# Second MLP product of a sixth round in three one-pass products, with a new order of all engines

## The chip, the cores and the metric

One core of one Trainium2 chip runs the kernel. The metric is the time of one execution in microseconds (us), as the median of several runs. Beside it stands one profiled execution, whose trace gives the start and the duration of each instruction on the five engines: PE (TensorE, matrix products), DVE (VectorE), ACT (ScalarE), POOL (GpSimd) and SP (SyncE, which here only issues transfers).

## What is computed

The reference is a linear attention followed by an MLP over each token:

```
# attention, per batch b and head h, with a state of 48 x 48
for t in range(S):                       # S = 768
    y[t] = r[t] @ (state + outer(u * k[t], v[t]))
    state = w[t][:, None] * state + outer(k[t], v[t])
# the 8 heads of 48 side by side give x: (4, 768, 384)
xn = (x - mean(x)) / sqrt(var(x) + 1e-6) * g_ln
out = x + maximum(xn @ w_ch1, 0) @ w_ch2     # w_ch1: 384 x 1536, w_ch2: 1536 x 384
```

All of it is in FP32.

## The kernel before

The work is cut into 8 rounds (`NR`), each of one batch and 384 of its tokens. A round has a *front*, the attention, and a *back*, the MLP.

**The front** forms products of decays in blocks that double in length (`quads`, `grow`, `keep`; tiles `k`, `r`, `tot`, and `A` for the 64 x 64 blocks of attention weights), most of it elementwise work on DVE with many small matrix products on PE between. The operands arrive as `nat_w`, `nat_k`, `nat_r` and `v`; `inner` multiplies them on DVE or POOL into `pad_k`, `pad_r`, `nat_k` and `nat_r`. At the end of a front `states` scans the states (`s`, and `last` for the next round; 10 small DVE instructions per group of four heads), `outputs` multiplies them with `r` on PE, and a copy by ACT or DVE leaves the round's rows in `x`.

**The back** normalises `x`, turns it (`xT_ps`, `xf`), and for 12 slabs `f` of the hidden layer forms `h` (`h_ps`, ReLU by ACT). Two ways of forming a product are used:

- FP32 as the engine has it. It is used for the first product of round 0 (`first_product`, tiles `w1` and `xf`), and for the second product (`o`, against `ffn2`) of the rounds below `LAST`: 3 row tiles times 12 slabs, 36 products per round.
- Three products in `fp32r`, one pass each. Both operands are split into a high and a low part, and into a scaled difference of the two, each exact in the shorter format (names ending in `H`, `L`, `D`). It is used for the first product of rounds 1 to 7 (parts `xhl` and `xd`, or `xk` and `xr`, against `wh`, `wl` and streamed `d`), and for the second product of the rounds from `LAST` on (`thirds`: 108 products per round, with `hH` by ACT, `hL` by DVE or POOL, `hD` by DVE, against the parts of `w_ch2` that `halve2` forms once as `w2H`, `w2L`, `w2D`).

`LAST` is 3, so rounds 3 to 7 use `thirds`. The parts of `w_ch2` are 36 slabs of 128 x 384 and have no room of their own. `w2_place` puts them into buffers that the fronts leave: `k`, `r`, `A`, `v`, `vx`, `tot`, `nat_k`, `nat_r` (tags `k`, `r`, `A`, `v`, `vx`, `tot`, `nk`, `nr`). Therefore the first `thirds` product of a round waits until the fronts of all rounds are done:

```
            if first:
                need += x_of(NR - 1)
```

The rounds' `x` lie in four buffers; `x_tag` puts that of round 7 into the buffer of `nat_w`. `h` has 12 buffers (tag `h`).

**The order.** `Plan.order` goes through a list of numbers, `ORDER`, one for each step of the kernel. It fixes the order of the instructions on every engine, and for steps that two engines can do (`EITHER`) the ten-thousands pick the engine. No engine reorders anything. Where the list leaves PE without a ready step for over 0.35 us by the plan's own account, `order` puts in products of zeros (`idle`), in whole pieces of 128 columns:

```
            if idle and e == "PE" and t - free["PE"] > 0.35:
                early = max(min(t - 0.1, self.WARMED) - free["PE"], 0.0)
                n = int(early / idle[1] / 2 + (t - 0.1 - free["PE"] - early) / idle[1])
```

All engine calls pass through one helper, so the profile names line 47 for nearly all of them; the tiles' names tell them apart.

Of the kernel before, what the change touches and what calls it, by code (L numbers as in the profile page):

```python
# [63 lines left out]
class Plan:  # L64
# [294 lines left out]
def kernel(  # L359
# [140 lines left out]

    BY = {"DVE": DVE, "POOL": POOL}
    EITHER = ("DVE", "POOL")
    THREE, LAST = 1, NR - 5

    def at(rnd, stage):
        return 40 * rnd + stage
# [617 lines left out]
    def x_tag(rnd):  # L1124
        return "x" if rnd < NR - 1 else "nw"
# [279 lines left out]
    def w2_place(n, f):  # L1405
# [4 lines left out]
        if f < 6:  # L1410
            return ("nk", "nr")[f - 4], f"xw2_{f}", 3, i
# [413 lines left out]
```

## Time and profile before

| what | us |
|---|---|
| median of 3 runs | 469.05 (468.63 to 470.08) |
| the profiled execution, its own time | 469.36 |
| its span, first to last instruction | 467.6 |
| PE busy | 459.7 (98%) |
| DVE busy | 352.5 (75%) |
| ACT busy | 264.5 (57%) |
| POOL busy | 139.1 (30%) |

The own time exceeds the span by 1.76 us, for what lies before the first and behind the last instruction. The span can be read in two parts: up to about 300 us the fronts run, with backs of rounds 0 to 3 between them; behind that PE does one-pass products alone. A PE that is shown busy can still be slow, since the records of a product overlap the next one; what a product costs is read from the distance of the starts.

### The profile page before, as it was taken

How to read it: one execution, taken by the hardware profiler on the slowest of the kernel's cores; microseconds unless marked ns; L12 is line 12 of the kernel's file. 1: busy time of each engine (PE TensorE's matmuls, PEld its weight loads, DVE VectorE, ACT ScalarE, POOL GpSimd, SP SyncE). 2: the span in 40 equal slices, each digit the busy share in tenths (PEclk: the TensorE clock that was granted, in tenths of full speed). 3: DMA queues.
4: the chain of work that ended last, by engine and by line, in shares of the span. 5: the costliest groups of instructions: out<-in, count | busy, mean ns of one | idle time of the engine just before them, and what ended most of it. 6: DMA issues, size and time to landing. Idle time of an engine off the chain costs nothing.

```text
span 467.6 us, 17460 instructions
## 1 busy us (share of the span) xinstructions
PE 459.7 (98%) x7442; PEld 400.8 (86%) x7442; DVE 352.5 (75%) x742; ACT 264.5 (57%) x608; POOL 139.1 (30%) x141
## 2 busy tenths in 40 slices
PE   9999999999999999999999999999999999999996
PEld 5766888766899766899766899999999999999996
DVE  8999899999997768897879887976633535525535
ACT  4697889754674332665621678855555455544440
POOL 4237014322361152363443230221013122321030
PEclk9999999999999999999999999999999999999999
DMA  7889765885657606844630545312212232142011
GB/s 207 248 199 240 203 124 144 239 212 139 180 160 162 133 4 151 185 128 127 170 66 4 86 123 133 105 32 69 84 55 70 80 102 67 37 135 68 35 50 51
DMA packets 105501, 56.23 MB, mean 120 GB/s; under 512 B 61904, under 2 KB 102352, under 8 KB 105424
## 3 DMA queue, kind: packets, MB, share of 16 engines
q1 hardware_dynamic: 105152, 54.92, 45.9%
q8 instruction: 58, 0.95, 0.9%
q10 hardware_dynamic: 272, 0.20, 0.1%
q14 instruction: 19, 0.16, 0.1%
HBM read 45.27 MB, written 7.47 MB: 113 GB/s over the span
## 4 chain that ended last, share of the span: by engine, by line
PE 86%; DVE 6%; DMA 3%; ACT 2%; POOL 2%; issue 1%; DVEq 0%; SPq 0%; POOLq 0%; ACTq 0%
PE h_ps L47 28%; PE a L47 25%; PE o L47 15%; PE o_2P L47 4%; PE idle L47 3%; PE r_ps L47 2%; PE k_ps L47 2%; PE o_2D L47 2%; DMA raw<-in_moe_w_ch_dram 2%; PE kn_ps L47 2%; PE xT_ps L47 2%; DVE s L47 1%; ACT held L47 1%; DMA va<-own_d 1%; POOL nat_k L47 1%
## 5 line engine op out<-in xcount | busy, mean ns | idle before, releaser
L47 ACT ACTIVATE h<-h_ps 128x384 f32<-128x384 f32 (+2 forms) x108 | 47.9, 457 | 50.5 <-PE h_ps L47 49.8
L47 PE MATMUL o<-ffn,h 128*128 128x384 f32 x216 | 74.6, 491 | 0.0
L47 DVE SCALAR_TENSOR_TENSOR hD<-hH,hL 128x384 fp32r<-128x384 f32 x60 | 36.4, 617 | 37.1 <-POOL hL L47 16.0
L47 POOL TENSOR_TENSOR hL<-h,hH 128x384 fp32r<-128x384 f32 x28 | 30.2, 1084 | 102.7 <-PE a L47 27.7
L47 ACT ACTIVATE h_ps<-h_ps 128x384 f32<-128x384 f32 x84 | 39.7, 480 | 34.5 <-PE h_ps L47 33.4
L47 PEld LDWEIGHTS o<-ffn,h 128*128 128x128 f32 x216 | 39.2, 190 | 23.0
L47 PEld LDWEIGHTS a<-r,k 48*56 48x56 f32 (+3 forms) x3072 | 40.0, 122 | 10.8 <-issue 5.2
L47 PE MATMUL h_ps<-xd,d 128*128 128x384 f32 x204 | 47.1, 335 | 0.0
L47 PE MATMUL a<-r,k 48*56 48x32 f32 (+3 forms) x3072 | 44.2, 208 | 1.0 <-issue 0.7
L47 PE MATMUL h_ps<-xhl,wl 128*128 128x384 f32 x180 | 40.4, 334 | 0.0
L47 DVE TENSOR_TENSOR r<-r,tot 112x768 f32<-112x768 f32 (+1 forms) x40 | 32.3, 809 | 9.6 <-PE a L47 9.6
L47 PE MATMUL h_ps<-xhl,wh 128*128 128x384 f32 x180 | 39.1, 326 | 0.0
L47 DVE TENSOR_TENSOR k<-k,tot 112x768 f32<-112x768 f32 (+1 forms) x40 | 31.6, 791 | 6.7 <-PE a L47 4.7
L47 ACT ACTIVATE hH<-h 128x384 fp32r<-128x384 f32 x60 | 29.7, 519 | 11.6 <-PE a L47 7.8
L47 PEld LDWEIGHTS h_ps<-xd,d 128*128 128x128 f32 x204 | 34.0, 189 | 0.5
L47 DVE TENSOR_TENSOR hL<-h,hH 128x384 fp32r<-128x384 f32 x32 | 18.0, 569 | 20.0 <-PE a L47 9.5
L47 PEld LDWEIGHTS h_ps<-xhl,wh 128*128 128x128 f32 x180 | 30.8, 189 | 0.0
L47 PE MATMUL idle<-nought 128*128 128x384 f32 (+2 forms) x90 | 29.6, 452 | 0.9 <-DVE eps L47 0.9
L47 ACT COPY A<-a 32x384 f32<-32x384 f32 (+5 forms) x56 | 23.6, 422 | 11.9 <-DVE xhl L47 5.6
L47 PEld LDWEIGHTS h_ps<-xhl,wl 128*128 128x128 f32 x180 | 30.1, 189 | 0.2
L47 PE MATMUL a<-w2D,hD 128*128 128x384 f32 x90 | 29.7, 330 | 0.4 <-DVE hD L47 0.4
L47 ACT ACTIVATE xf<-xT_ps,g_sb 128x384 f32<-128x384 f32 (+2 forms) x27 | 14.7, 550 | 22.1 <-PE xT_ps L47 19.0
(184 smaller groups left out, 1136.9 us busy)
## 6 DMA issues: line engine op xcount, KB each, us to landing
d<-w1d SPq DMA_DIRECT2D x84, 192.0 KB, 2.6
raw<-in_moe_w_ch_dram SPq DMA_DIRECT2D x24, 384.0 KB, 4.6
nat_w<-in_w_dram SPq DMA_DIRECT2D x24, 192.0 KB, 4.0
nat_r<-in_r_dram SPq DMA_DIRECT2D x24, 192.0 KB, 4.0
v<-in_v_dram SPq DMA_DIRECT2D x24, 192.0 KB, 4.1
nat_k<-in_k_dram SPq DMA_DIRECT2D x23, 192.0 KB, 4.1
out_dram<-x SPq DMA_DIRECT2D x15, 192.0 KB, 2.0
w1d<-w1diff SPq DMA_DIRECT2D x12, 192.0 KB, 2.3
```

Of the source, the lines that this page charges most:

```text
L47: ins = self.tc.keep_in_program_order(f(*args, **kw))
```

## The change

- `LAST` becomes 2: round 2 too uses `thirds`. Its second product is 108 one-pass products in place of 36 FP32 products; its `h` is split by ACT, DVE and POOL; each of its three row tiles gets two additions on DVE in place of one, and its rows are stored by three transfers in place of one.
- The buffer of `nat_k` takes `x` of round 6, so that rounds 2 to 7 all have room for `x` while they wait. The parts of slab 4 of `w_ch2` that stood there move to three buffers of the tag `h`, which leaves nine for `h` itself.
- The parity in `x_places` follows `LAST`: rounds 3, 5 and 7 put their parts into `xk` and `xr`, before it was rounds 4 and 6.
- `ORDER` is another list, so that every engine has another order, and some steps another engine.

```
     ORDER = [
-        10008, 3, 2, 10012, 4, 9, 10, 5, 11, 16, 264, 261, 7, 14, 13, 18, 10019, 262, 17, 265, 260, 263,
...
+        4, 3, 2, 11, 7, 9, 10, 12, 13, 5, 263, 260, 261, 262, 16, 10018, 19, 264, 265, 269, 14, 17, 21,
...
     EITHER = ("DVE", "POOL")
-    THREE, LAST = 1, NR - 5
+    THREE, LAST = 1, NR - 6
...
     def x_tag(rnd):
-        return "x" if rnd < NR - 1 else "nw"
+        return {NR - 2: "nk", NR - 1: "nw"}.get(rnd, "x")
...
         if f < 6:
-            return ("nk", "nr")[f - 4], f"xw2_{f}", 3, i
+            return ("nr", "xw2_5", 3, i) if f == 5 else ("h", f"w2{n}_4", 1, 0)
```

260 rows, old and new, of the table ORDER are left out of this document.

## The prediction

> **What bounds the kernel now.** I read the page first: the span, the busy times and the slices.
>
> ```profile
> span 467.6 us, 17460 instructions
> PE 459.7 (98%) x7442; PEld 400.8 (86%) x7442; DVE 352.5 (75%) x742; ACT 264.5 (57%) x608; POOL 139.1 (30%) x141
> PE   9999999999999999999999999999999999999996
> DVE  8999899999997768897879887976633535525535
> PE 86%; DVE 6%; DMA 3%; ACT 2%; POOL 2%; issue 1%; DVEq 0%; SPq 0%; POOLq 0%; ACTq 0%
> ```
>
> PE is busy everywhere and carries 86% of the chain that ended last, so the kernel is bound by PE. But the DVE slices show a second candidate: 9 nearly throughout the first 12 slices (140 us), 7 and 8 until about 300 us, then 3 to 6. Next I cut the span into stages by windows (PE, PEld, DVE, ACT, POOL busy, then PE's granted clock); the cuts at 297.4 and 299.7 us are explained below.
>
> ```profile
> 0.00:10.00 10.00, 9.07 (x22) 5.41 (x23) 7.73 (x24) 4.15 (x5) 5.33 (x16) 1.00 0.69 203
> 10.00:60.00 50.00, 47.95 (x1043) 37.72 (x1042) 47.73 (x117) 40.17 (x102) 17.03 (x17) 1.00 0.82 216
> 60.00:140.00 80.00, 80.00 (x1513) 64.70 (x1511) 77.96 (x160) 57.49 (x136) 27.60 (x24) 1.00 0.68 175
> 140.00:297.40 157.40, 157.29 (x3730) 129.17 (x3724) 129.53 (x276) 78.64 (x177) 53.72 (x51) 1.00 0.50 114
> 299.70:463.00 163.30, 162.88 (x1013) 161.49 (x1005) 85.69 (x162) 81.74 (x186) 35.28 (x33) 1.00 0.22 66
> ```
>
> From 60 to 140 us DVE is busy 77.96 of 80 us (97.5%); from 140 to 297.4 us 129.53 of 157.4 (82%): there PE's products set the pace and DVE has slack. Behind the fronts DVE needs 85.69 of 163.3 us, half. So there are two regimes, a front stage with two engines near their limit and a back stage of PE alone. The timeline gives the hinges: the last state scan on DVE, the last attention product on PE, PE's last product, and the last addition.
>
> ```profile
> 296.82 0.61 DVE L47 SCALAR_TENSOR_TENSOR s<-s,decay,a 112x48 f32<-112x48 f32 x3
> 299.34 0.46 PE L47 MATMUL a<-s,r 48*64 48x48 f32 x18
> 462.89 0.33 PE L47 MATMUL a<-w,hH 128*128 128x384 f32 x1
> 463.95 0.62 DVE L47 SCALAR_TENSOR_TENSOR x<-a,rstd,x 128x384 f32<-128x384 f32 x1
> ```
>
> DVE ends the scans at 297.4 us, PE the fronts at 299.7 us (2.3 later), PE its last product at 463.1 us (163.4 later), and 4.5 us remain for additions and the store. 299.7 + 163.4 + 4.5 = 467.6. The change is costed as a shift of the first two terms.
>
> **The product itself.** From the chain in order of time, for the price of one product, and from the groups of line, engine and form, for the fillers:
>
> ```profile
> 239.84 3.89 PE o L47 x12
> 440.31 3.90 PE h_ps L47 x24
> L47 PE MATMUL o<-ffn,h 128*128 128x384 f32 x216 | 74.6, 491 | 0.0
> L47 PE MATMUL idle<-nought 128*128 128x384 f32 x44 | 20.2, 582 | 0.9 <-DVE eps L47 0.9
> ```
>
> An FP32 product leaves two records (216 for 3 rounds of 36), so 12 records in 3.89 us are 6 products of 0.648 us. A one-pass product leaves one record: 24 in 3.90 us, 0.1625 us each. Round 2 gives up 36 x 0.648 = 23.3 us and takes 108 x 0.1625 = 17.55 us: PE gains 5.8 us.
>
> **Fillers.** The changed order holds 54 products of zeros (116 pieces of 128 columns), before 45 (97 pieces). A piece is a third of a 384-column FP32 product, 0.216 us: 19 more cost 4.1 us. Where they stand matters more. Before, all lie ahead of PE's first `h_ps`. Now 23 pieces, at nine places, stand in the middle, from the end of round 1's `o` to round 6's products with `A`: the order itself finds no product there, since round 2's second product, which could fill, must now wait for the last front. The code puts in whole pieces and leaves 0.1 to 0.34 us at each place, so 0.9 to 3.1 us of waiting stay uncovered; I take 2.
>
> **What moves.** Counted in the two orders, PE has this ahead of the last attention product: `o` products 108 before, 72 after; one-pass `h_ps` 318 before, 210 after (round 3 had 102 of its 108 there; now only round 2's stand there, less a last piece); transposes 9 fewer, about 1 us; attention products equal. So 23.3 + 108 x 0.1625 + 1.0 - 4.1 = 37.7 us less PE work ahead of that hinge, and 216 x 0.1625 + 1.0 = 36.1 us more behind it. By PE alone the fronts end at 299.7 - 37.7 + 2 = 264.0 us.
>
> DVE is the question, for the fronts are the same work and must fit into that shorter stage. Until the last scan it was busy 7.73 + 47.73 + 77.96 + 129.53 = 263.0 us. The largest differences of its list until that scan, with these prices:
>
> ```profile
> L47 DVE COPY_PREDICATED A<-mask,a 128x768 f32<-128x768 int8 x18 | 17.9, 992 | 4.6 <-PE a L47 4.6
> L47 DVE TENSOR_TENSOR nat_r<-pad_k,pad_r 128x576 f32<-128x576 f32 x9 | 7.9, 882 | 0.4 <-POOL pad_r L47 0.4
> L47 DVE SCALAR_TENSOR_TENSOR x<-o,rstd,x 128x384 f32<-128x384 f32 x9 | 5.4, 609 | 2.1 <-PE o L47 2.1
> L47 DVE COPY x<-a 128x288 f32<-128x288 f32 x11 | 5.0, 451 | 1.1 <-PE a L47 1.1
> L47 DVE TENSOR_TENSOR nat_k<-nat_k,nat_r 128x1152 f32<-128x1152 f32 x3 | 4.1, 1352 | 0.1
> L47 DVE TENSOR_SCALAR xn<-x,mv 128x384 f32<-128x384 f32 x8 | 3.2, 415 | 0.0
> L47 DVE TENSOR_TENSOR pad_k<-nat_k,nat_w 128x576 f32<-128x576 f32 x2 | 1.5, 748 | 0.0
> ```
>
> Three masked copies, three `nat_r`, three `x<-o`, five `x<-a` and five `xn` go (to ACT, to POOL, or behind the scan): 2.98 + 2.65 + 1.83 + 2.26 + 2.08 = 11.8 us. Four `nat_k` products and four `pad_k` products come from POOL: 5.41 + 2.99 = 8.4 us. The other differences are a few instructions of each of two dozen kinds, by estimate 5 to 9 us fewer. That leaves 263.0 - 8.3 to 263.0 - 12.4: 250.6 to 254.7 us of DVE work. After the first 10 us (7.73 busy, loads arriving) 242.9 to 247.0 us remain. At the 97.5% of the 60-to-140 stage they take 249.1 to 253.3 us, the scan ends at 259.1 to 263.3 us, and PE's last attention product at 261.4 to 265.6 us. At 95.5%, the 47.73 of 50 us of the stage before, it is 266.6 to 270.9 us; with DVE never idle 255.2 to 259.3 us, and then PE's 264.0 holds.
>
> So both engines want 264 us, each to run there without slack, and each waits for the other: PE gets scans and masked copies from DVE, DVE gets blocks from PE. Before, neither had to: DVE idled 18% in the longer half of the fronts. I take 265.0 us, one more than PE's figure, inside DVE's band.
>
> **The burst behind the fronts.** `thirds` starts almost at once now: 1.3 us of PE work after the last attention product, 5.2 before. It needs splits of `h` and of `w2`, about 0.55 us from start to start:
>
> ```profile
> 301.98 0.63 DVE L47 SCALAR_TENSOR_TENSOR w<-w,ffn 128x384 fp32r<-128x384 f32 x1
> 302.54 0.68 DVE L47 SCALAR_TENSOR_TENSOR w2L<-w2H,ffn 128x384 fp32r<-128x384 f32 x1
> DVE hD L47 <- POOL hL L47: 16.0, 8, 3.3
> L47 POOL TENSOR_TENSOR hL<-h,hH 128x384 fp32r<-128x384 f32 x28 | 30.2, 1084 | 102.7 <-PE a L47 27.7
> ```
>
> From the last scan to `hD` of slab 3 DVE has 21 instructions, 11.5 us; PE has 7.7 us of products ahead of that slab and starts 2.3 us later. It waits 1.5 us there; by slab 6 DVE has caught up. Before, slab by slab, PE's work exceeded DVE's, and the stage lost 2 us in all. I add 1 us: 163.4 + 36.1 + 1.0 = 200.5 us. If DVE also waits for POOL's `hL`, as 8 times before for 2 us each, it is up to 4 us more.
>
> **Hidden.** ACT's 12 more `hH`, three more additions and the three short stores lie in the back stage, where ACT is busy 81.74 and DVE 85.69 of 163.3 us. 5 of the 24 new `hL` and `hD` go to POOL. Nine buffers for `h` in place of 12 cost nothing while ACT splits each `h` soon; else PE waits for a free `h`. Round 6's rows must wait until round 7 has used up `nat_k`; that copy stands near the end of the fronts anyway. If these covers go, each costs its wait of 0.5 to 2 us.
>
> **The sum.** 265.0 + 200.5 + 4.5 = 470.0 us of span, 2.4 more than 467.6. Against its own time that is 471.8 (469.36 + 2.4), against the median of the runs 471.4 (469.05 + 2.4; the profiled execution stood 0.3 above it).
>
> **Rivals.** (1) *The gain comes through.* DVE runs gapless, the splits are ready, and the nine edges vanish, since the real waits are shorter than the plan's: PE's ledger alone, 262.0 + 199.5 + 4.5 = 466.0, so 467.4 at the median, or 466 if the front's fewer handovers save another 1 to 1.5 us. For: 97.5% was held for 80 us. Against: the order's own fillers say that PE has nothing to do. (2) *It cancels.* PE's ledger with its 2 us of edges, DVE just keeps up, the burst costs nothing: 264.0 + 199.5 + 4.5 = 468.0, 469.5 at the median. (3) *The burst decides, slower.* Fronts at 265.0, but `hD` waits for POOL and ACT in the first six slabs: 3 to 4 us on top, 475. It decides from the point where slab 6 still finds PE waiting. (4) *The clock falls in the thinned front.* The windows show a granted clock of 1.00 in every stage, so no stage here is slow; if it halved for the about 10 us around the fillers, of which by estimate half is products that PE must do, they would take some 5 us longer: 476. Against: fillers stand at just these places.
>
> The Trainium skill, page "TensorE: Matmul & The Clock Gate", section "HAM oscillation — how this bites in real kernels", warns of idle gaps over about 3.4 us, after which the clock is halved; by that rule the fourth rival needs one gap of that length, and the trace shows none so far.
>
> (5) That the change does not do what it says is excluded: the built order holds 648 one-pass `thirds` products, 540 before.
>
> **How the numbers follow.** Forecast 0.43, rival 1 0.22, rival 2 0.20, rival 3 0.12, rival 4 0.03. 0.3% (1.4 us) is about what a measurement of this kernel can tell from no change: faster means below 467.6, slower above 470.5. Rival 1 gives faster 0.20; rival 2, with the edges of 1 and of the forecast, gives 0.23 within; the rest, 0.57, is slower. The range goes from 465.5 (rival 1 with a little more) to 476.5 (DVE at 95.5%: 268.8 + 200.5 + 4.5 = 473.8, so 475.3; or the burst).
>
> **What would show it.** Right: the last attention product between 263 and 268 us; DVE at 96% or more until then; PE waiting for DVE or POOL between its fillers at 170 to 230 us and in the first slabs of round 2's `thirds`; then some 199 to 201 us of dense products. Wrong, faster: the fronts end by 262 us and DVE's idle share stays below 2%. Wrong, slower: waits for `h` buffers, or gaps, in the back stage, which I count as dense.

## The result, and the profile after

The changed kernel takes 480.8 us (median of four runs, 478.6 to 482.2) against 469.6 us before (four runs, one more than ahead of the prediction): a ratio of 1.0233, with a 95% interval of [1.0212, 1.0255]. All ratios leave out the runs of a second, slower state (three of the kernel before with less PE work, one of the version with eight waits). The prediction was 471.4, with a range up to 476.5. The profiled execution took 480.1 us by its own time, with a span of 478.4 us where 470.0 was predicted. From its page, in the order of the prediction:

```profile
span 478.4 us, 17626 instructions
PE 460.9 (96%) x7496; PEld 408.5 (85%) x7496; DVE 362.8 (76%) x751; ACT 281.4 (59%) x648; POOL 125.9 (26%) x141
PE   8998999999999989998998999999999999999996
DVE  6999999999996998999996994564733463542535
PE 67%; DVE 20%; ACT 5%; SPq 3%; DMA 2%; issue 2%; ACTq 0%; DVEq 0%
```

PE is no longer 9 throughout: five slices ahead of the hinge show an 8, and DVE is at 9 nearly until the fronts' end. Of the chain that ended last, PE carries 67% (86% before) and DVE 20% (6%). The *hinge* is the end of the fronts: the last state scan on DVE and, behind it, the last attention product on PE. The windows (PE, PEld, DVE, ACT, POOL busy, then the granted clock of PE):

```profile
10.00:60.00 50.00, 46.12 (x1021) 35.62 (x1020) 48.27 (x115) 42.41 (x105) 15.38 (x18) 1.00 0.83 225
60.00:140.00 80.00, 78.56 (x1463) 62.55 (x1463) 79.16 (x148) 54.07 (x129) 26.17 (x25) 1.00 0.68 169
140.00:200.00 60.00, 58.42 (x1554) 46.30 (x1546) 53.01 (x112) 29.11 (x66) 23.55 (x24) 1.00 0.55 130
200.00:272.40 72.40, 67.75 (x2089) 58.57 (x2082) 66.81 (x148) 45.13 (x103) 18.91 (x23) 1.00 0.45 98
275.50:474.10 198.60, 198.48 (x1238) 197.61 (x1230) 104.11 (x203) 102.46 (x235) 37.54 (x35) 1.00 0.23 68
```

The timeline's hinges: the last scan, the last attention product, the last product, the last addition.

```profile
270.88 1.49 DVE L47 SCALAR_TENSOR_TENSOR s<-s,decay,a 112x48 f32<-112x48 f32 x8
275.15 0.46 PE L47 MATMUL a<-s,r 48*64 48x48 f32 x18
473.91 0.33 PE L47 MATMUL a<-w,hH 128*128 128x384 f32 x1
474.97 0.62 DVE L47 SCALAR_TENSOR_TENSOR x<-a,rstd,x 128x384 f32<-128x384 f32 x1
```

The last scan ends at 272.4 us, the fronts on PE at 275.5, PE's products 198.6 us later, and 4.3 us remain. Predicted were 265.0 + 200.5 + 4.5. So the fronts are 10.5 us late, and the back stage is 1.9 us better than predicted; it is dense (198.48 of 198.60 us busy). All of the miss of this execution lies ahead of the hinge. Its granted clock is 1.00; two of the other three executions had a mean of 0.991 and 0.993 and took 482.2 and 481.5 us, while those at 1.000 took 480.1 and 478.6. So 1 to 2 us of the median may be the clock.

### The profile page after: what moved, and what is told of

Same layout as the page of the kernel before. It is cut to its first block, busy times and chain, and to the rows that moved or that the text cites. A ratio compares the mean times of both kernels' runs of the same rounds, so it can differ in the third digit from the quotient of the medians.

```text
span 478.4 us, 17626 instructions
## 1 busy us (share of the span) xinstructions
PE 460.9 (96%) x7496; PEld 408.5 (85%) x7496; DVE 362.8 (76%) x751; ACT 281.4 (59%) x648; POOL 125.9 (26%) x141
## 4 chain that ended last, share of the span: by engine, by line
PE 67%; DVE 20%; ACT 5%; SPq 3%; DMA 2%; issue 2%; ACTq 0%; DVEq 0%
PE h_ps L47 27%; PE a L47 23%; PE o_2P L47 5%; PE o L47 4%; DVE A L47 4%; DVE nat_k L47 3%; SPq L47 3%; DVE s L47 2%; PE o_2D L47 2%; DVE k L47 2%; DVE vals L47 2%; DVE r L47 1%; PE r_ps L47 1%; PE xT_ps L47 1%; DMA nat_r<-in_r_dram 1%
## 5 line engine op out<-in xcount | busy, mean ns | idle before, releaser
L47 POOL TENSOR_TENSOR hL<-h,hH 128x384 fp32r<-128x384 f32 x33 | 37.2, 1132 | 144.1 <-ACT hH L47 66.7
L47 PE MATMUL o<-ffn,h 128*128 128x384 f32 x144 | 50.6, 491 | 0.0
L47 DVE TENSOR_TENSOR hL<-h,hH 128x384 fp32r<-128x384 f32 x39 | 21.5, 554 | 27.8 <-ACT hH L47 15.7
L47 ACT ACTIVATE hH<-h 128x384 fp32r<-128x384 f32 x72 | 36.3, 520 | 6.1 <-PE a L47 3.1
L47 PE MATMUL a<-w2D,hD 128*128 128x384 f32 x120 | 39.3, 327 | 0.0
L47 PEld LDWEIGHTS o<-ffn,h 128*128 128x128 f32 x144 | 25.8, 190 | 14.0 <-ACT tot L47 0.2
L47 PE MATMUL a<-w2L,hL 128*128 128x384 f32 x108 | 35.2, 326 | 0.0
L47 PE MATMUL a<-w2H,hH 128*128 128x384 f32 x108 | 35.2, 326 | 0.0
L47 PE MATMUL h_ps<-xhl,wl 128*128 128x384 f32 x144 | 32.1, 332 | 0.3
L47 PE MATMUL h_ps<-xhl,wh 128*128 128x384 f32 x144 | 31.2, 326 | 0.0
L47 PEld LDWEIGHTS idle<-nought 128*128 128x128 f32 x108 | 18.9, 197 | 9.3 <-issue 1.5
```

The lines of the kernel that those rows point to most:

```text
L47: ins = self.tc.keep_in_program_order(f(*args, **kw))
```

## Experiments

Two theories came first: A, that DVE's work now sets the fronts' end; B, that PE's order and its handovers do. The differences in us below are the difference of the ratio from 1.0233 (changed kernel) or from 1 (before), times 469.6 us.

### Less DVE work, and less PE work

Edit in both kernels (the product `nat_k` x `u`):

```
-            k_, k_, lambda: u_bc[...]..., 2 * half, 5,
+            lambda: k_()[..., 0:1], lambda: k_()[..., 0:1], lambda: u_bc[...]...[..., 0:1], 2 * half, 5,
```

> The changed kernel, with the product nat_k x u on one element in 48 of each row (it leaves out most of the product with u). Seven of these run on DVE inside the fronts, 1.35 us each for 1152 columns; at 24 columns by estimate some 1.18 us less each, 8.3 us less DVE work. Theory A (after the change DVE's work sets the fronts' end): the last scan comes 6 to 8.3 us sooner, the last attention product too, and the time falls from 480.8 to 472.5 to 475. Theory B (PE's own order and its handovers set it): the hinge stays at 275, 480 to 481.

> The kernel before with the same cut (most of the product with u is left out): six on DVE, about 7.1 us less DVE work, and one on POOL. Theory A: DVE had slack in the fronts before, so the time falls by at most 1.5 us, 468 to 469.5. Theory B: the same nothing, 469.5. If it falls by 5 us or more, DVE was the bound before as well and theory A's contrast is false.

The group in the changed kernel:

```profile
L47 DVE TENSOR_TENSOR nat_k<-nat_k,u_bc 128x1152 f32<-128x1152 f32 x7 | 10.2, 1461 | 0.0
```

Its group with the cut, and the last scan on the timeline then:

```profile
L47 DVE TENSOR_TENSOR nat_k<-nat_k,u_bc 128x24 f32<-128x24 f32 x7 | 2.1, 301 | 0.0
```

```profile
268.32 1.48 DVE L47 SCALAR_TENSOR_TENSOR s<-s,decay,a 112x48 f32<-112x48 f32 x8
```

8.1 us of this group went (DVE's busy time until the last scan fell by 7.7), the last scan came 2.6 us sooner (269.8), the ratio is 1.0173 [1.0109, 1.0236], 2.8 us, or 5.8 at the interval's lower end. The kernel before moved by 1.0 us (0.9979 [0.9943, 1.0015]). Theory A as stated falls: by the middle a third came through, not 6 to 8.3 us.

Edit for PE in both kernels (the second product of round 1):

```
-                    for f_ in range(f, f + KC):
+                    for f_ in range(f, f + KC, 2 if rnd == 1 else 1):
```

> The changed kernel with half of round 1's second MLP product left out (every second slab's FP32 products, 12 of 0.648 us: 7.8 us less PE work in the fronts). Theory A: DVE sets the fronts' end, the hinge moves by 0 to 3 us, time 478 to 481. Theory B: the hinge moves by all of it, time 473.

> The kernel before with the same half of round 1's second product left out (7.8 us less PE work in the fronts). Both theories: PE sets the fronts' end there, the time falls by 6 to 7.8 us, to 462 to 463.5. If it falls by less than 4 us, DVE was close behind PE before the change too.

Neither kernel gained: 1.0239 [1.0151, 1.0326] and 1.0009 [0.9971, 1.0047]. Theory B as stated falls as well, and so does what both theories expected of the kernel before. In the kernel before with the cut, waits come in place of the products. Its windows, and the longest wait on the timeline (in brackets the idle time ahead):

```profile
172.00:212.00 40.00, 34.21 (x853) 28.47 (x851) 34.29 (x75) 18.57 (x42) 14.88 (x15) 1.00 0.58 136
212.00:219.00 7.00, 6.57 (x100) 6.48 (x101) 5.26 (x9) 1.87 (x4) 4.21 (x5) 0.51 0.30 84
```

```profile
212.43 0.34 PE L47 MATMUL a<-v,A 64*64 64x48 f32 x1 [2.40 <-DVE last L47]
```

Without the cut PE was busy in all of these 40 us. Now 5.8 us of them are idle, at a granted clock of 1.00: four waits of over 0.9 us, three of which end with DVE, one with ACT. So most of the 7.8 us came back as waits, and behind the longest of them the granted clock is 0.51 for 7 us. Over 0 to 310 us such losses add up to some 5.2 us in this execution and 5.1 us in the changed kernel with the cut (one minus the granted clock, summed over windows of 10 us; an estimate, as if PE were always waited for). The clock alone is not the reason: this execution took 475.9 us, but the two of ten whose mean clock was 1.000 took 468.0 and 472.0, no clear gain over 470.3 either. Some of what PE did here thus lay beside waits for DVE, in the kernel before too.

### POOL's hold on DVE

The changed kernel's timeline showed where DVE's time goes:

```profile
223.23 1.40 POOL L47 TENSOR_TENSOR nat_r<-pad_k,pad_r 128x576 f32<-128x576 f32 x1
224.00 3.05 DVE L47 COPY_PREDICATED A<-mask_own,va 128x768 f32<-128x768 int8 x1
224.59 0.22 POOL L47 TENSOR_TENSOR decay<-tot 112x24 f32<-112x24 f32 x1
224.77 1.39 POOL L47 TENSOR_TENSOR nat_r<-pad_k,pad_r 128x576 f32<-128x576 f32 x1
```

The masked copy takes 1.02 us where POOL is idle. Here it starts within a POOL product, sees it end at 224.63, and itself ends only after a second one, at 227.05, 0.9 us behind that one's end. Three more copies were stretched. The expectation below says that they end together with a POOL product; by the trace they end 0.6 to 0.9 us behind one. Theory C: POOL holds DVE, and this is a good part of the 10 us; theory D: it counts for a third, as other DVE work did. Edits: POOL's step waits for the copy beside it (first), and POOL's products of rounds 1 to 7 cut to one element in 48, except those that open a buffer (second, in both kernels):

```
+                others |= {x.i for x in (beside,) if x and x.own}
...
+            ).own = True
```

```
+                if e == "POOL" and rnd and not new:
+                    to = to[..., 0:1]
+                    a, b = (x if x.shape[-1] == 1 else x[..., 0:1] for x in (a, b))
```

> The changed kernel, in which a POOL product that stands beside DVE's masked copy of v waits until that copy is done (the computation is whole). In the changed kernel four such copies lasted 1.73 to 3.05 us in place of 1.02, each ending together with a POOL product. Theory C (DVE is held by POOL, and that is a good part of the 10 us that the fronts are late): the copies take 1.02 us, about 5 us of DVE time is saved, and the time falls by 2 to 5 us, to 476 to 479. Theory D (the fronts' end is set by a chain of handovers in which DVE's time counts for about a third, as the cut product with u let 2.8 of 8.3 us through): 1 to 2 us at most, 479 to 480.

> The changed kernel with POOL's products of k, r and w in rounds 1 to 7 cut to one element in 48 (some 22 products of 0.8 to 1.3 us by DVE's price, up to 2.6 on POOL; it leaves out most of these products). They can hold DVE no longer and their results come early. Theory C: all of the stretch goes (about 9 us of DVE time in the fronts), 4 to 9 us sooner, 472 to 477. Theory D: a third of it and what waits for POOL, 2 to 4 us sooner, 477 to 479. If nothing moves, neither POOL's results nor its hold on DVE count.

> The kernel before with the same cut of POOL's products in rounds 1 to 7 (20 products; most of them is left out). About 7 us of stretch in the fronts goes. Theory C: DVE has slack there, at most 1.5 us, 468 to 469.5. Theory D: a little, 0 to 3 us, 466.5 to 469.5.

The first gave 1.0184 [1.0169, 1.0198], 2.3 us, but it did not do what it was meant to: the copy at 224 us shrank to 1.50 us only, others stayed, and their mean hardly moved (1273 ns), so it tells little, and where its 2.3 us come from is open. The second: the group of copies in the changed kernel, then with the short products, and the last scan on the timeline:

```profile
L47 DVE COPY_PREDICATED A<-mask_own,va 128x768 f32<-128x768 int8 x14 | 18.1, 1304 | 2.2 <-ACT A L47 2.2
L47 DVE COPY_PREDICATED A<-mask_own,va 128x768 f32<-128x768 int8 x14 | 14.2, 1021 | 2.2 <-ACT A L47 2.2
```

```profile
261.99 1.48 DVE L47 SCALAR_TENSOR_TENSOR s<-s,decay,a 112x48 f32<-112x48 f32 x8
```

The copies fell from a mean of 1304 ns (18.1 us for 14) to 1021 ns, DVE was busy 7.9 us less until the last scan with the same instructions, the scan ended 8.9 us sooner (263.5), and the ratio is 1.0094 [1.0074, 1.0114], 6.5 us. That is theory C. The kernel before gained 0.3 us (0.9993 [0.9983, 1.0003]), but it is no equal contrast. Its group of copies, without and with the short products:

```profile
L47 DVE COPY_PREDICATED A<-mask_own,va 128x768 f32<-128x768 int8 x14 | 15.2, 1088 | 0.0
L47 DVE COPY_PREDICATED A<-mask_own,va 128x768 f32<-128x768 int8 x14 | 15.3, 1094 | 0.0
```

The copies were little stretched there, and did not get shorter; DVE's busy time until the last scan fell by 2.1 us (263.0 to 260.9) and not by the expected 7, since the products left whole still held DVE (a copy at 198 us took 2.01 us beside one of them). So it stays open what 7 us of hold would be worth in the kernel before.

Short products also deliver sooner, so two kinds of edit were made in which they do not. In one, named POOL steps wait for the DVE steps that they held (four, then eight of them); the computation is whole:

```
+    for late, copy in ((478, 335), (673, 508), (1043, 978), (1230, 1167)):
...
+        plan.ops[late].after.append(plan.ops[copy])
```

> The changed kernel; the four POOL products beside which DVE's masked copy of v was stretched (at 42, 80, 170 and 224 us, 0.7 to 2.0 us longer than the 1.02 us of one alone, 4.8 us in all) are put behind that copy and wait for it; the computation is whole. If DVE's being held is what the run with short POOL products won: the four copies take 1.02 us, DVE is busy some 4.8 us less until the last scan, and 2 to 4.5 us come through, 476 to 478.5. If it was that POOL's results came sooner (each product there took 1.4 us or more on POOL): nothing is won, or up to 2 us lost, since these four start later, 480.5 to 483.

> The same for all eight places in which DVE is held 0.7 us or more (also nat_k x u at 37, w1diff at 117, k at 122 and r at 163 us; 8 us in all). By the hold: 3 to 6.5 us sooner, 474 to 477.5. By POOL's results: no gain, 480 to 484.

With four, the group of copies, then the timeline:

```profile
L47 DVE COPY_PREDICATED A<-mask_own,va 128x768 f32<-128x768 int8 x14 | 14.2, 1020 | 2.2 <-ACT A L47 2.2
```

```profile
222.03 1.01 DVE L47 COPY_PREDICATED A<-mask_own,va 128x768 f32<-128x768 int8 x1
267.52 1.48 DVE L47 SCALAR_TENSOR_TENSOR s<-s,decay,a 112x48 f32<-112x48 f32 x8
```

The copies are at 1.02 us in the mean, the scan ends at 269.0, and the ratio is 1.0152 [1.0126, 1.0178]: 3.8 us won although POOL starts later. It is the fastest of the versions here that leave nothing out, and still behind the kernel before. Eight did not win more (1.0162 [1.0136, 1.0189]): a copy at 168 us, free in the first version, then took 2.03 us. A hold that was avoided by waiting turned up elsewhere. The last edit keeps POOL as busy and its results as late, but lets it read nothing:

```
+                if e == "POOL" and rnd and not new:
+                    for part_ in (to, to, to[..., 0:16]):
+                        POOL.memset(part_, 0.0)
+                    return
```

> The changed kernel; POOL's products of k, r and w in rounds 1 to 7 are replaced by fills of the same tile with zeros, two whole and one of a third (it leaves out these products). By the fill of 384 columns in 0.42 us that is some 1.4 us in place of the 1.4 to 1.5 us of a product of 576, so POOL's results come as late as before, but it reads nothing. If DVE is held by POOL's reading of two operands, and that is what the short products won: the masked copies take 1.02 us, the last scan comes 7 to 9 us sooner, time 472 to 474.5. If the early results won it: masked copies may be short, but the last scan comes 0 to 4 us sooner, time 477 to 481. If a fill holds DVE as a product does, the copies stay stretched and the run does not tell.

Its page, two of its groups, and the last scan on the timeline:

```profile
PE 459.3 (97%) x7496; PEld 408.1 (87%) x7496; DVE 355.6 (75%) x751; ACT 281.5 (60%) x648; POOL 125.1 (27%) x185
```

```profile
L47 POOL MEMSET nat_r<- 128x576 f32 x16 | 9.2, 578 | 1.8 <-DVE nat_k L47 1.3
L47 DVE COPY_PREDICATED A<-mask_own,va 128x768 f32<-128x768 int8 x14 | 14.2, 1022 | 2.2 <-ACT A L47 2.2
```

```profile
264.02 1.48 DVE L47 SCALAR_TENSOR_TENSOR s<-s,decay,a 112x48 f32<-112x48 f32 x8
```

POOL is busy 125.1 us, 125.9 before the edit; DVE 355.6 instead of 362.8; the scan ends at 265.5, 6.9 us sooner; the ratio is 1.0070 [1.0041, 1.0098], 7.7 us. The masked copies take 1.02 us though fills run beside them. So what these 6.9 us hang on is the hold, not the time at which POOL delivers.

The Trainium skill, page "SBUF — State Buffer", section "Who interferes with whom", says that a DVE instruction with two inputs in SBUF contends with a GpSimd instruction that reads SBUF, not with one that only writes it. The runs agree: 3.05 us beside products, 1.02 us beside fills.

The kernel's plan has an account of this: steps that it marks `port` wait for one another across DVE and POOL (`held` in `Plan.order`). The step of these masked copies, `place_own`, is not marked in either kernel, so the plan counts them as free of POOL. No run made the order anew with the mark.

### The fillers, and the one-pass products

Edits: the zero products behind the first 60 us of the plan left out, alone and together with the short POOL products; and FP32 products in place of 30 of round 2's 36 triples.

```
+                    if t < 60:
                         out.append(lambda n=n, home=home: idle[2](n, home[1]))
```

> The changed kernel without the 23 pieces of zero products that stand behind the first 60 us (5.0 us of PE). If the fillers themselves delay the fronts (they are longer than the waits that they fill): 2 to 5 us sooner, 476 to 479. If they lie in waits: no change, 480 to 481. If the granted clock falls without them, as it fell to 0.83 to 0.95 in five slices of 10 us of the run that left out 7.8 us of products in this stage: 2 to 8 us later, 483 to 489, with the low clock at 170 to 260 us.

> The changed kernel with POOL's products in rounds 1 to 7 cut to one element in 48 (most of them is left out), and without the 23 pieces of zero products behind the first 60 us. Alone the first won 6.5 us and the second 1.9 (4.0 in the fronts of its profiled execution, with the granted clock at 0.91 from 200 to 260 us). If the two are separate causes of the late fronts they add up: the last attention product at 262 to 264 us, time 465 to 469, level with the kernel before or sooner. If both remove the same waits: 471 to 474. If the clock falls as in the run without fillers, 1 to 3 us of it are lost.

> The changed kernel and its order, with 30 of round 2's 36 triples of one-pass products replaced by one FP32 product of the high part each (it leaves out the low part and the difference in these). By the prices 30 x (0.648 - 3 x 0.1625) = 4.8 us more PE work behind the fronts. If the back stage is PE's alone, as the prediction had it, 4.5 to 5 us later, 485 to 486; if the three products also cost splits or waits that an FP32 product would not, less, down to no difference.

Without fillers alone, windows and the last scan on the timeline:

```profile
214.00:216.00 2.00, 0.32 (x24) 0.33 (x28) 2.00 (x3) 1.73 (x4) 0.00 (x0) 1.00 0.74 94
216.00:222.00 6.00, 6.00 (x184) 5.66 (x180) 4.43 (x10) 3.19 (x7) 2.91 (x4) 0.50 0.46 109
```

```profile
267.10 1.49 DVE L47 SCALAR_TENSOR_TENSOR s<-s,decay,a 112x48 f32<-112x48 f32 x8
```

The clock fell to 0.50 behind a gap of 1.71 us, and yet 1.9 us were won (1.0192 [1.0171, 1.0214]; the interval just overlaps that of the changed kernel's). That need not be the fillers' own cost: the order in time shifted, and the 14 masked copies took 15.7 us in place of 18.1 in this execution, so part of the gain may be less hold. Together with the short products it was 1.0126 [1.0096, 1.0155], 1.5 us slower by the middle than the short products alone (the intervals overlap): the two do not add up. In that execution the granted clock was 0.83, 0.63 and 0.86 in the three windows of 10 us from 210 us on, and the last scan came at 269.2 us, 5.7 later than with the short products alone. The third run on the timeline:

```profile
277.13 0.46 PE L47 MATMUL a<-s,r 48*64 48x48 f32 x18
480.56 0.33 PE L47 MATMUL a<-w,hH 128*128 128x384 f32 x1
```

Its back stage lasts 203.3 us, 4.7 more than the changed kernel's 198.6, where 4.8 was expected; the time moved by 6.2 us (1.0365 [1.0333, 1.0397]), since the fronts ended 2.0 us later in this execution too, with a clock of 0.83 in two windows of 10 us. The price of the products in the prediction holds: FP32 would cost in the back stage what the ledger says.

### More work

One of every three FP32 products of round 1 is followed by a product of zeros into the same place; or the sums of `nat_k` are formed twice.

```
+                        if rnd == 1 and f_ % 3 == 1:
+                            PE.matmul(tiles[o], zeros, nought.broadcast_to([P, RN]), start=False, stop=False)
```

```
+                    if kind == 0:
+                        DVE.tensor_reduce(out=steps(tiles[name][...]), in_=products(), axis=AX.X, op=ALU.add)
```

> The changed kernel with 12 products of zeros of 0.648 us added to round 1's second product (7.8 us more PE work in the fronts, added to the sums as zeros; the computation is whole). If PE's work sets the fronts' end one for one, as the prediction's ledger has it: 7 to 8 us later, 487 to 489. If the fronts' end is set by handovers and DVE, and PE's products lie partly in waits: 3 to 6 us, 483.5 to 486.5. If DVE alone sets it: 0 to 2 us.

> The kernel before with the same 12 products of zeros (7.8 us). PE was 98% to 100% busy in its fronts, so by the ledger 7 to 8 us later, 476.5 to 477.5. If the work that was left out before won nothing because PE's products lie in waits there too: 2 to 6 us, 471 to 475.

> The changed kernel with the first of DVE's sums over nat_k done twice (eight more reductions into the same place, about 1.27 us each for 1152 columns, some 9 to 10 us more DVE work in the fronts; the computation is whole). If DVE's work sets the end: 8 to 10 us later, 489 to 491. If it counts for about a third, as the cut did: 3 us, 483 to 485. A mixed chain, where work added counts for more than work removed: 5 to 8 us, 486 to 489.

> The kernel before with the same eight reductions done twice (9 to 10 us more DVE work). DVE had 32 us of idle time there: 0 to 3 us later, 469.5 to 472.5. If it is 6 us or more, the fronts of the kernel before hung on DVE too, and the contrast between the two kernels is only one of degree.

| added | changed kernel | kernel before |
|---|---|---|
| 7.8 us on PE | 1.0476 [1.0445, 1.0507], 11.4 us later | 1.0268 [1.0241, 1.0295], 12.6 us later |
| some 11 us on DVE | 1.0455 [1.0401, 1.0509], 10.4 us later | 1.0199 [1.0141, 1.0257], 9.3 us later |

The kernel before with the sums formed twice, their group, and the last attention product on the timeline:

```profile
L47 DVE TENSOR_REDUCE vals<-nat_k 128x24 f32<-128x1152 f32 x14 | 18.9, 1351 | 0.2
```

```profile
306.82 0.46 PE L47 MATMUL a<-s,r 48*64 48x48 f32 x18
```

Its fronts end at 307.3 us, 7.5 later, though DVE had been idle for 34 us there. The price of 11 us is from this group (18.9 in place of 9.4) and the smaller ones of the first round. What was expected of the kernel before (0 to 3 us) was wrong. Work added on either engine reaches the end nearly whole or more, while work taken away alone wins little: an idle share of 18% was no slack. Whether that is because both engines stand at a limit, or because the added steps lie on a chain of handovers, no run separates. The prices are not clean: with PE's addition, and in the changed kernel with DVE's, the clock fell in places (0.65 and 0.67 from 20 to 40 us with DVE's). But the one execution of the kernel before with more PE work whose clock was 1.000 took 481.5 us, still 11.8 more.

## Why the prediction was wrong

**The product, the back stage, the tail: right.** 198.6 us measured for 200.5; the burst behind the fronts cost nothing (the 1 us added for it was not needed), no `h` buffer was waited for, and the FP32 run confirmed the price of the products. The granted clock is 1.00 in every window of the profiled execution, so rival 4 did not happen in it; in two of the other three a mean clock of 0.991 and 0.993 may have cost 1 to 2 us. The runs with less PE work and without fillers show how near it was: gaps of 2.40 and 1.71 us were followed by 7 and 6 us at half clock. By the rule of 3.4 us that the prediction named from the Trainium skill these gaps would have been harmless; the measurement decides.

**The failed step is the fronts' term, 265.0 us; it was 275.5.** In it, DVE's work came out and the waits did not. DVE's busy time until the last scan was 254.3 us, inside the band of 250.6 to 254.7. But after the first 10 us DVE was busy 94.2% of the time (247.25 of 262.4 us), not 97.5%. At 97.5% that work would have ended at 263.6 us; the scan ended at 272.4, and 8.8 of its 9.7 us of lateness (262.7 would have given 265.0) are this share. The prediction saw that both engines had to run without slack and that each waits for the other, and then gave those waits 1 us ("264 on both, so 265"). It had read the 82% of before as slack that could be used up; the runs with added DVE work show that it was not. The share held up to 140 us (48.27 of 50 and 79.16 of 80 us) and fell behind that, where 12.6 of the 15.2 idle us lie. The longest of DVE's waits from 10 to 272.4 us, as engine, tile and what it waited for, then us in total, times, and the longest:

```profile
DVE k L47 <- PE a L47: 4.4, 3, 3.0
DVE r L47 <- PE a L47: 3.1, 4, 1.9
DVE A L47 <- ACT A L47: 2.2, 1, 2.2
```

So DVE waited mostly for PE, the handover that the prediction had named and priced too low. What makes just these waits no experiment separates.

**Beside the waits, the runs showed a cost that the prediction did not know: POOL's hold.** It named POOL's results as a possible wait, in the burst, but no hold on DVE in the fronts. DVE is busy 7.9 us less until the last scan with short products, 7.1 with fills, and the scan comes 8.9 and 6.9 us sooner (263.5 and 265.5, just above the predicted band of 259.1 to 263.3). DVE's idle time hardly changes by it:

```profile
10.00:272.40 262.40, 250.85 (x6093) 203.05 (x6092) 247.25 (x519) 170.73 (x400) 84.01 (x89) 1.00 0.62 151
10.00:265.50 255.50, 249.62 (x6096) 202.99 (x6094) 240.45 (x519) 170.75 (x400) 83.52 (x134) 1.00 0.63 155
```

With fills (second line) the share is 94.1%, as low as without. So the hold is a cost of some 7 us on top of the waits. Without it the changed kernel takes 472.9 us by the ratio, within the range and still slower than before.

**That the busy time fell inside the band is in part luck.** The band was worked out with durations of the kernel before, and these hold such stretches too. By an estimate (each DVE instruction less the shortest of its form, where it runs beside POOL, from 10 us to the last scan) they are some 7 us before and 9.5 us after. What changed more is where they lie: on the masked copies `A<-mask_own,va` 1.3 us before and 5.5 us after. Without the hold the busy time would have been 246.4 to 247.3 us, 3 to 4 below the band.

**PE's ledger.** 37.7 us of products were taken off one for one. The cut of round 1's products shows that such work lay in part beside waits for DVE; taking it away leaves the wait (5.8 us of 7.8 came back so). The changed order puts fillers, 5.0 us of them, where it expects waits. The 2 us for edges may have been too small: without these fillers the scan came 3.8 us sooner, though some of that may be less hold.

**Rivals.** None of them was this. Rival 3 named POOL, at another place and through another wait. The upper end of the range stood for DVE at 95.5%; it was 94.2%, with the hold counted as busy. Rival 1's argument, that 97.5% was held for 80 us, did not carry over behind 140 us.

**Open.** Why a cut of 8.1 us in the product with `u` won 2.8 us and 7 to 8 us of hold won 6.5 to 7.7 is not known. Both feed the attention weights `A`: the sums over that product (`vals`) go by two transfers into `va`, which the masked copies place. No run separates them.

## What to carry to other kernels

A hold of one engine by another counts as busy time, so a busy share does not show it. Before a change moves work between DVE and POOL, look for instructions of the one that begin while the other runs and take longer than the shortest of their group, and price them by the difference. An idle share is not slack: add a little work to each engine and see what comes out at the end before counting on it. Work taken off an engine in a stage of handovers may only uncover waits, and if the engine is PE a fall of the clock may follow the uncovered wait.

## What the runs showed of the hardware

POOL's product of two tiles in SBUF held a masked copy on DVE (data and mask from SBUF) for 0.7 to 2.0 us, the longest copy being 3.05 us in place of 1.02; fills on POOL of the same tiles, beside such copies, held nothing (mean 1022 ns). One masked copy was held by two POOL products in turn. Gaps on PE of 2.40 us (kernel before with less PE work) and 1.71 us (changed kernel without fillers) were followed by a granted clock of 0.51 for 7 us and of 0.50 for 6 us; a gap of 1.69 us early in the changed kernel with less DVE work was followed by no fall, so the length alone does not decide.
